# A second expert's first matrix is loaded one unit earlier, and two steps beside it change places

## The chip, the cores and the metric

The kernel runs on one core of one Trainium2 chip. The metric is device microseconds of one execution, from launch to end; several runs are taken and their median is compared. A profile is one further execution, recorded instruction by instruction. Engines are named PE (TensorE), DVE (VectorE), ACT (ScalarE), POOL (GpSimd) and SP (SyncE, which here only issues DMAs).

## What is computed

Attention with a compressive memory feeds two mixture-of-experts layers, one after the other. All tensors are float32, N is 2304 tokens, D 512, F 1024, and each layer has 8 experts. The first layer sends each token to one expert, the second to two; the cut below leaves the attention out.

```python
def _moe_ref(x, modality_id, w_gate, modality_bias, w1, w2):
    logits = x @ w_gate + modality_bias[modality_id]
    e_idx = np.argmax(logits, axis=1)
    ...
    for e in range(E):
        mask = e_idx == e
        h = np.maximum(x[mask] @ w1[e], 0.0)
        out[mask] = gate_w[mask, None] * (h @ w2[e])
    return out

def _moe2_ref(x, w_gate, w_noise, noise, w1, w2):
    noisy_logits = x @ w_gate + np.log1p(np.exp(x @ w_noise)) * noise
    top2 = np.argpartition(-noisy_logits, 2, axis=1)[:, :2]
    ...
    for e in range(E):
        for k in range(2):
            mask = top2[:, k] == e
            h = np.maximum(x[mask] @ w1[e], 0.0)
            out[mask] += top2_w[mask, k, None] * (h @ w2[e])
    return out

x = attn_out as (B*S, 512); x = _moe_ref(x, ...); return _moe2_ref(x, ...)
```

## The kernel before

The attention fills the first quarter of the span. Its instructions are ordered by a planner (class Tasks), and unit 0 of the first layer is planned in with them. From unit 1 on the order on every engine is that in which the Python code stands.

A **unit** of the first layer is 256 tokens of one expert (`full`). Both weights of an expert are 2 MB each. They are loaded raw (tiles w1r and w2r), and every float32 operand is split into a high and a low part: ACT casts the high one (w1h, w2h, xh), and DVE or POOL subtracts it to get the low one (w1l, w2l, xl). A product is then three matmuls per block (lines 718 to 720 and 728 to 730). The first product goes through eight blocks f of 128 hidden columns. The second goes through two token tiles t and four quarters q of the hidden columns; a quarter is six matmuls of 512 columns. In a unit the parts of the next unit's w1 are split during the second product (`split_w1`, one call per quarter), and the next tokens are gathered from DRAM by POOL and transposed by PE (`rows`, which calls `xsplit`: four transposes, ACT's xh, DVE's xl, and before a pair also ACT's unsplit copy xf).

**Between unit 1 and unit 2** stands `pair`: two halves t of 128 tokens each, of two experts, with unsplit float32 weights and tokens (tile xf). The first half uses w1r and w2r; the second half uses weights of another expert, wb1 and wb2. wb1 lies where unit 1 holds w2h and wb2 where it holds w2l. While the second half runs, w1r is loaded with unit 2's w1 and split. The code has four pairs, each inside an `If` on a register that counts them. In this run the first pair is done; the branch of the second is taken on every engine and jumps over the code of the other three. At the end of the jump each engine adds to its semaphores what the skipped code would have added, and unit 2 waits for these.

**Ranking.** The outputs of each unit get the second layer's gate logits and a rank among the tokens of the same expert. This work (`logits`, `route2`) is for the unit before the one that runs. `route2` is a generator: each `pump(slot)` runs up to five pieces of it. Slots 0 to 7 are the blocks f of the first product, slots 8 to 15 the quarters of the second (slot 8+4t+q). After the routing mask A is made on DVE (line 916) the generator yields 1, and `pump` then does nothing until the slot GATE[1], which is 10; the next piece is PE's five small matmuls on A (lines 919 to 923).

In the pair the slots are counted likewise: 8t+q in the first product of half t, 8t+4+q in the second.

Of the kernel before, what the change touches and what calls it, by code (L numbers as in the profile page):

```python
# [291 lines left out]

EARLY=256; CH=(C2-DEAD)//2
OLP=8
LSLOT=(0,1,3); GATE={1:10,2:99}; PUMP=5
LSLOT2=(0,1,2); GATE2={1:6,2:10}; PUMP2=8
AREAS=(9216,9216,5120,10240,8192,GB*XW,2*XW,512)

# [9 lines left out]
class Moe:  # L308
# [41 lines left out]
    def blocks(s, nc, c, areas):  # L350

        def T(j, o, w, name, dt=FT):
            assert o+w<=AREAS[j]
            return nc.alloc_sbuf_tensor_at(name,[128,w],dt,offset=nc.lookup_mloc(areas[j]).addr+4*o).ap()
        cut=lambda j,o,w,name,n,dt=FT:[T(j,o+i*w,w,name+str(i),dt) for i in range(n)]
        V=lambda a,k: a.rearrange('p (k w) -> p k w',k=k)
        K0,K1,X,HL,W2,G,X1,OL=range(8)
        s.w1r=V(T(K0,0,4096,'w1r'),KD); s.w2r=V(T(K0,4096,4096,'w2r'),KF); s.os=cut(K0,8192,512,'os',2)
        s.w1h=V(T(K1,0,4096,'w1h',FR),KD); s.w1l=V(T(K1,4096,4096,'w1l',FR),KD); s.yt=V(T(K1,8192,1024,'yt'),KD); s.rr=c.tile([128,4,256],FR,name='rrm')
        s.xh=V(T(X,0,2560,'xh',FR),KD); s.xl=V(T(X,2560,2560,'xl',FR),KD)  # L360
        s.w2h=cut(W2,0,512,'w2h',KF,FR); s.w2l=cut(W2,4096,512,'w2l',KF,FR)
        H=lambda n: [T(HL,o,KF*n,x+str(n),FR).rearrange('p (f c) -> p f c',f=KF) for o,x in ((0,'hh'),(5120,'hl'))]
        s.hidden=dict(l1=H(UT),l2=H(C2)); s.hh,s.hl=s.hidden['l1']
        s.xf=[V(T(X,o,2560,n),KD)[:,:,256:512] for o,n in ((0,'xf0'),(2560,'xf1'))]; s.hf=T(HL,0,KF*UT,'hf').rearrange('p (f c) -> p f c',f=KF)
        s.wb1=V(T(W2,0,4096,'wb1'),KD); s.wb2=V(T(W2,4096,4096,'wb2'),KF)
        s.x1=V(T(X1,0,2*XW,'x1'),2); s.ol2=V(T(OL,0,512,'ol2',FR),4); s.gs=cut(G,0,XW,'gs',GB); s.gn_=s.on_=0
        s.room=lambda o,w,dt: T(G,2*XW+o,w,'room%d'%o,dt); s.room1=lambda o,w,dt: T(X,o,w,'roox%d'%o,dt)
        t=KF*UT; s.tail=[T(HL,t,NT*128,'tl',FR),T(HL,5120+t,NT*3*COLS,'tr',FR),T(HL,5120+t+NT*3*COLS,NT*COLS,'to')]; s.ob=T(HL,5120,5120,'ob')
        s.kv=[T(X,2560,2560,'k0'),T(HL,0,2560,'k1')]; s.vs=[T(X,0,2560,'v0'),T(HL,2560,2560,'v1')]
        s.mask=T(G,2*XW,800,'mask'); s.mzs=T(G,2*XW+800,520,'mzs')  # L370
        s.bufs=dict(q=cut(HL,5120,512,'q',4),qb=cut(HL,7168,512,'qb',2),pts=cut(HL,8192,1024,'pts',2)+cut(W2,3328,1024,'ptx',1),
            sm=cut(W2,0,576,'sm',4),ph=cut(W2,2304,512,'ph',2),p=cut(W2,4352,640,'p',4),os=[T(K1,8192,512,'oc')],x=cut(W2,6912,512,'x',2),
            mo=cut(X1,0,512,'mo',2),xt=[T(OL,0,512,'xt')],l=cut(G,2*XW+1320,32,'l',3))
# [70 lines left out]
    def tasks(s, Q, A, w1, w2):  # L444
# [240 lines left out]
        Q.add(P+14,POOL,100,lambda:nc.gpsimd.memset(s.x1[:,:,D:],0.0),b3['x_add']+end)  # L685
        Q.add(P+14,POOL,300,lambda:nc.gpsimd.memset(s.rr[:,:,4*NC2:].bitcast(FT),0.0))

    def load_w(s, raw, w, e, eng=None):
        src=(w[bass.ds(e,1)] if not isinstance(e,int) else w[e:e+1]).rearrange('o (c p) f -> p (o c) f',p=128)
        (eng or s.nc.sync).dma_start(raw,src)  # L690
# [114 lines left out]
    def full(s, wk, ps, w1, w2, u):  # L805
        nc=s.nc; V=nc.vector
        e=s.expert(1,0) if u==1 else s.expert(0,u-1); s.load_w(s.w1r,w1,e)
        s.finish(); s.x1_out(s.np*2+2 if u==2 else col(u-1),2)
        s.chain=s.route2(wk,ps,u-1,2); s.hold=0
        nc.gpsimd.tensor_copy(s.nz[:,1],s.nz[:,0])  # L810
        for f in range(KF):
            s.mm1(ps,f,0,UT)
            if u==1: s.late(f)
            elif f==1: s.behind()
            if u>=NSTAT-1:
                if f==1:
                    last=s.last[:,u-1:u]
                    V.tensor_scalar(s.nx[:,0],s.M2[:,0,0:2],float(S0),0.0,op0=OP.add,op1=OP.max)
                    V.tensor_scalar(s.nx[:,1],s.nx[:,0],float(N),last,op0=OP.add,op1=OP.mult)
                    V.tensor_add(s.nxi,s.nx[:,1],s.gn[:,u-1])  # L820
                    V.tensor_scalar(s.run[:,0:1],last,float(EARLY),s.run[:,0:1],op0=OP.mult,op1=OP.max)
                if f==2: g=[s.gather(s.xd[:N+col(u-1)*128],s.nxi[:,t:t+1]) for t in range(2)]
            elif f==(7 if u==1 else 0): g=[s.gather(s.xd[:N],(s.gsi[:,0] if u==1 else s.gni[:,u-1])[:,t:t+1]) for t in range(2)]
            if f in LSLOT: s.logits(wk,ps,1+LSLOT.index(f))
            s.split_w(s.w2r,s.w2h,s.w2l,f,nc.vector if f<3 else nc.gpsimd)
            if f>LSLOT[2]: s.pump(f)
            if f==5: nc.gpsimd.tensor_copy(s.gwc,s.gws[:,col(u)+1:col(u)+2])
            if f==7: s.split_w1(0,nc.gpsimd)
        s.load_w(s.w2r,w2,e)
        for t in range(2):  # L830
            for q in range(4):
                y=s.mm2(ps,t*128,range(2*q,2*q+2),y if q else None)
                i=4*t+q
                if i<7: s.split_w1(i+1,nc.vector if i in (1,3,6) else nc.gpsimd)
                if i in ((3,5) if u==1 else (1,3)): s.rows(ps,i//4 if u==1 else i//2,g[i//4 if u==1 else i//2],s.xf[0] if u==1 else None)
                if t==1 and q==1: s.logits(wk,ps,0)
                s.pump(8+i)
                if i==6: s.kept(col(u),2)
            if not t: nc.scalar.activation(s.x1[:,0,:D],y,AF.Copy,scale=s.gws[:,col(u):col(u)+1])
        s.settle(y)  # L840
    def pair(s, wk, ps, w1, w2, p):


        nc=s.nc; V=nc.vector; G=nc.gpsimd; c0=HC+2*p
        e=s.expert(1,p+1); eb=s.expert(1,NP2+1+p)
        s.load_w(s.wb1,w1,eb)
        s.finish(); s.x1_out(c0-2,2)
        s.load_w(s.wb2,w2,eb)
        s.chain=s.route2(wk,ps,NF+p,2); s.hold=0
        G.tensor_copy(s.nz[:,1],s.nz[:,0])  # L850
        xf=s.xf[p%2]; g=[]
        for t,(a1,a2) in enumerate(((s.w1r,s.w2r),(s.wb1,s.wb2))):
            cs=slice(t*128,t*128+128)
            for q in range(4):
                if q%2==0: h=ps.tile([128,4,128],FT,name='h')
                for f in (2*q,2*q+1):
                    for k in range(KD): nc.tensor.matmul(h[:,f%4],a1[:,k,f*128:f*128+128],xf[:,k,cs],start=k==0,stop=k==KD-1)
                if q%2: nc.scalar.activation(s.hf[:,2*q-2:2*q+2,cs],h,AF.Relu)
                if t==0:
                    if q==1: s.behind(); g=[s.gather(s.xd[:N],s.gsi[:,p+1,j:j+1]) for j in range(2)]  # L860
                    if q in LSLOT: s.logits(wk,ps,1+LSLOT.index(q))
                if t and q:
                    for f in (2*q-2,2*q-1): s.split_w1(f,V if f%2 else G)
                if t or q>=LSLOT[2]: s.pump(8*t+q)
            if t==0: s.load_w(s.w1r,w1,e)
            y=ps.tile([128,512],FT,name='y')
            for q in range(4):
                for f in (2*q,2*q+1): nc.tensor.matmul(y,s.hf[:,f,cs],a2[:,f],start=f==0,stop=f==KF-1)
                if t:
                    if q==0:  # L870
                        for f in (6,7): s.split_w1(f,V if f%2 else G)
                elif q%2: s.rows(ps,q//2,g[q//2],s.xf[(p+1)%2])
                if t and q==0: s.logits(wk,ps,0)
                s.pump(8*t+4+q)
                if not t and q==1: G.tensor_copy(s.gwc,s.gws[:,c0+1:c0+2])
                if t and q==2: s.kept(c0,2)
            if not t: nc.scalar.activation(s.x1[:,0,:D],y,AF.Copy,scale=s.gws[:,c0:c0+1])
            if t==0: s.load_w(s.w2r,w2,e)
        s.settle(y)
# [287 lines left out]
```

## Time and profile before

| | us |
|---|---|
| median of 3 runs | 987.15 |
| lowest, highest | 986.49, 991.69 |
| the profiled execution | 984.86 |
| its span, first to last instruction | 983.1 |
| PE busy in the span | 943.0 |
| DVE busy | 555.5 |
| ACT busy | 488.2 |
| POOL busy | 353.2 |

Times below are microseconds from the start of the span of the profiled execution. Unit 1 runs from 248.8 to 284.6, the pair from there to 317.8, unit 2 after it. In the timeline views a row has the start, the time busy, the engine, the line of the kernel, the operation, the tiles written and read, the shapes and the count; a bracket at its end tells how long the engine stood idle before it and which instruction released it. A busy time runs over the start of the next instruction where an engine pipelines, so the cost of one instruction in a row of equal ones is the distance of two starts.

### The profile page before, as it was taken

Reading aid. Unit: us, or ns where it says so; the run is one execution under the profiler, and the core shown is the slowest. Engines: PE = TensorE matmul, PEld = TensorE weight load, DVE = VectorE, ACT = ScalarE, POOL = GpSimd, SP = SyncE. Lnnn points to the kernel's source line nnn. Section 1 sums busy time; section 2 is a strip of 40 time slices with the busy share of each in tenths; the row PEclk is TensorE's granted clock in tenths of the full one; section 3 lists DMA queues with packets and bytes.
Section 4 is the critical chain, followed back from the end, with each engine's and each line's share of the span. In section 5 each row is a group of like instructions: output and inputs, shape, how many; then the busy total and the mean of one; then the engine's idle time right before and its main releaser. Section 6 shows DMA issues by size and latency. Waiting matters only on the chain. (4 is left out here: it accounts for less than half of the span.)

```text
span 983.1 us, 18583 instructions
## 1 busy us (share of the span) xinstructions
PE 943.0 (96%) x6849; PEld 831.0 (85%) x6849; DVE 555.5 (56%) x1695; ACT 488.2 (50%) x1141; POOL 353.2 (36%) x420
## 2 busy tenths in 40 slices
PE   7999999999989999999997999999999999999994
PEld 5888888888875889888886999898989989898983
DVE  8777777789745577777775244243442424244320
ACT  6887878775433455555552244333342433343320
POOL 5222232244643567777765231121313021231111
PEclk9999999999989899999999999999999999999997
DMA  8345856262567555666655254536446354535112
GB/s 211 100 112 183 270 184 205 93 223 84 167 214 265 162 193 206 216 215 215 205 178 158 66 137 124 127 82 160 105 107 172 97 121 128 138 77 117 23 23 35
DMA packets 83840, 144.98 MB, mean 147 GB/s; under 512 B 14480, under 2 KB 32912, under 8 KB 83728
## 3 DMA queue, kind: packets, MB, share of 16 engines
q1 hardware_dynamic: 73168, 117.10, 36.4%
q0 software_dynamic: 10560, 26.47, 13.6%
q8 instruction: 60, 0.98, 0.4%
q14 instruction: 52, 0.43, 0.1%
HBM read 111.65 MB, written 31.97 MB: 146 GB/s over the span
## 5 line engine op out<-in xcount | busy, mean ns | idle before, releaser
L718 PE MATMUL b<-xh,w1h 128*128 128x304 f32 (+3 forms) x800 | 240.0, 300 | 3.1 <-ACT xh L709 1.3
L719 PE MATMUL b<-xl,w1h 128*128 128x304 f32 (+3 forms) x800 | 238.2, 298 | 3.8 <-DVEq L788 3.5
L720 PE MATMUL b<-xh,w1l 128*128 128x304 f32 (+3 forms) x800 | 237.1, 296 | 0.0
L723 DVE SCALAR_TENSOR_TENSOR hl<-b,hh 128x304 fp32r<-128x304 f32 (+3 forms) x200 | 90.7, 454 | 207.1 <-ACT hh L721 205.4
L728 PE MATMUL b<-w2h,hh 128*128 128x512 f32 x464 | 188.7, 407 | 0.0
L730 PE MATMUL b<-w2h,hl 128*128 128x512 f32 x464 | 182.2, 393 | 0.0
L973 POOL DMA_INDIRECT out_dram<-os,l2s x40 | 62.8, 1571 | 331.5 <-ACT os L972 253.3
L729 PE MATMUL b<-w2l,hh 128*128 128x512 f32 x464 | 181.6, 391 | 0.0
L721 ACT ACTIVATE hh<-b 128x304 fp32r<-128x304 f32 (+3 forms) x200 | 81.8, 409 | 172.7 <-PE b L720 172.6
L718 PEld LDWEIGHTS b<-xh,w1h 128*128 128x128 f32 x800 | 152.7, 191 | 9.3 <-DVE hl L723 4.1
L719 PEld LDWEIGHTS b<-xl,w1h 128*128 128x128 f32 x800 | 152.7, 191 | 4.8 <-DVEq L788 3.7
L720 PEld LDWEIGHTS b<-xh,w1l 128*128 128x128 f32 x800 | 152.9, 191 | 0.0
L730 PEld LDWEIGHTS b<-w2h,hl 128*128 128x128 f32 x464 | 87.5, 189 | 19.5
L729 PEld LDWEIGHTS b<-w2l,hh 128*128 128x128 f32 x464 | 88.0, 190 | 15.5
L728 PEld LDWEIGHTS b<-w2h,hh 128*128 128x128 f32 x464 | 87.7, 189 | 15.4
L151 ACT ACTIVATE p<-sm,l 128x128 f32<-128x128 f32 (+4 forms) x144 | 84.1, 592 | 16.9 <-DVE l L147 16.9
L698 DVE TENSOR_TENSOR w1l<-w1r,w1h 128x512 fp32r<-128x512 f32 x84 | 71.3, 857 | 22.0 <-ACT w1h L697 21.8
L710 DVE TENSOR_TENSOR xl<-b,xh 128x512 fp32r<-128x512 f32 x56 | 38.6, 689 | 73.9 <-ACT xh L709 73.7
L693 ACT CAST w2h<-w2r 128x512 fp32r<-128x512 f32 x128 | 78.5, 613 | 0.0
L709 ACT CAST xh<-b 128x512 fp32r<-128x512 f32 x56 | 32.9, 587 | 87.7 <-PE b L708 87.7
L697 ACT CAST w1h<-w1r 128x512 fp32r<-128x512 f32 x128 | 74.7, 620 | 0.3 <-DMA w1r<-in_w_dram 0.3
L972 ACT ACTIVATE os<-b,l2w 128x512 f32<-128x512 f32 x40 | 27.7, 691 | 94.1 <-PE b L730 47.6
(460 smaller groups left out, 1511.4 us busy)
## 6 DMA issues: line engine op xcount, KB each, us to landing
w1r<-in_w_dram SPq DMA_DIRECT2D x18, 2048.0 KB, 9.6
w2r<-in_w_dram SPq DMA_DIRECT2D x18, 2048.0 KB, 9.2
xd<-gs SPq DMA_DIRECT2D x24, 260.0 KB, 3.7
xd<-x SPq DMA_DIRECT2D x10, 520.0 KB, 10.3
out_dram<-gs SPq DMA_DIRECT2D x19, 256.0 KB, 4.0
k<-in_k_dram SPq DMA_DIRECT2D x16, 256.0 KB, 4.3
q<-in_q_dram SPq DMA_DIRECT2D x16, 256.0 KB, 3.5
v<-in_v_dram SPq DMA_DIRECT2D x16, 256.0 KB, 4.4
```

The source lines that it names most:

```text
L151: s.nc.scalar.activation(s.P[b,i,u][:,lh*n:lh*n+n],s.SM[b,i,u][:,lh*n:lh*n+n],AF.Exp,scale=-1.0,bias=L[:,0,c:c+1],accum_out=L[:,1,c:c+1])
L693: nc.scalar.copy(hi[c],raw[:,c])
L697: nc.scalar.copy(s.w1h[:,:,fs],s.w1r[:,:,fs])
L698: eng.tensor_sub(s.w1l[:,:,fs],s.w1r[:,:,fs],s.w1h[:,:,fs].bitcast(FT))
L718: nc.tensor.matmul(h[:,:n],s.w1h[:,k,fs],s.xh[:,k,cs],start=k==0,stop=False)
L719: nc.tensor.matmul(h[:,:n],s.w1h[:,k,fs],s.xl[:,k,cs],start=False,stop=False)
L720: nc.tensor.matmul(h[:,:n],s.w1l[:,k,fs],s.xh[:,k,cs],start=False,stop=k==KD-1)
L721: def mm1_a(s, h, f, c0, n): s.nc.scalar.activation(s.hh[:,f,c0:c0+n],h[:,:n],AF.Relu)
L723: cs=slice(c0,c0+n); s.nc.vector.scalar_tensor_tensor(s.hl[:,f,cs],h[:,:n],0.0,s.hh[:,f,cs].bitcast(FT),op0=OP.max,op1=OP.subtract)
L728: nc.tensor.matmul(y,s.hh[:,f,cs],s.w2h[f],start=f==0,stop=False)
L729: nc.tensor.matmul(y,s.hh[:,f,cs],s.w2l[f],start=False,stop=False)
L730: nc.tensor.matmul(y,s.hl[:,f,cs],s.w2h[f],start=False,stop=f==KF-1)
```

## The change

- The pair's wb1 gets a place of its own: two tiles of two k-blocks each in area HL (at 2048 and 7168), where unit 1's first product keeps tables (tl, tr) that its ranking of the first layer has read by then. For the first pair its load, now two DMAs of 1 MB, is issued in unit 1 right behind the load of w2r. Later pairs load it where they did. wb2 stays where it was.
- In the pair's second half, the calls `split_w1(f)` for unit 2's w1 follow the two blocks f of the same q, where they followed one q later, and the last two came after the first quarter of the second product. Six of the eight subtractions go to DVE (two to POOL: f = 0 and 4), where it was four and four.
- Unit 1 pumps its ranking by GATE1, with 12 where GATE has 10.

```diff
-LSLOT=(0,1,3); GATE={1:10,2:99}; PUMP=5
+LSLOT=(0,1,3); GATE={1:10,2:99}; GATE1={1:12,2:99}; PUMP=5
...
-        s.wb1=V(T(W2,0,4096,'wb1'),KD); s.wb2=V(T(W2,4096,4096,'wb2'),KF)
+        s.wb1=[V(T(HL,o,2048,'wb1%d'%o),2) for o in (2048,7168)]; s.wb2=V(T(W2,4096,4096,'wb2'),KF)
...
+    def load_wb1(s, w, e):
+        src=w[bass.ds(e,1)].rearrange('o (c p) f -> p (o c) f',p=128)
+        for i,x in enumerate(s.wb1): s.nc.sync.dma_start(x,src[:,2*i:2*i+2])
...
-            if f>LSLOT[2]: s.pump(f)
+            if f>LSLOT[2]: s.pump(f,GATE1 if u==1 else GATE)
...
         s.load_w(s.w2r,w2,e)
+        if u==1: s.load_wb1(w1,s.expert(1,NP2+1))
...
-                s.pump(8+i)
+                s.pump(8+i,GATE1 if u==1 else GATE)
...
-        s.load_w(s.wb1,w1,eb)
+        if p: s.load_wb1(w1,eb)
...
-                if t and q:
-                    for f in (2*q-2,2*q-1): s.split_w1(f,V if f%2 else G)
+                if t:
+                    for f in (2*q,2*q+1): s.split_w1(f,V if f%4 else G)
...
-                if t:
-                    if q==0:
-                        for f in (6,7): s.split_w1(f,V if f%2 else G)
-                elif q%2: s.rows(ps,q//2,g[q//2],s.xf[(p+1)%2])
+                if not t and q%2: s.rows(ps,q//2,g[q//2],s.xf[(p+1)%2])
```

PE in unit 1, around the five ranking matmuls. b is a PSUM bank, hh, hl and w2h, w2l are the split operands of the second product, gs a gathered token tile and x the outputs whose logits are made. Before:

```order
L730 MATMUL b_157<-w2h_74,hl_86 128x512
...
L919 MATMUL b_161<-A_3437,trib 128x8
...
L728 MATMUL b_157<-w2h_75,hh_85 128x512
...
L730 MATMUL b_157<-w2h_76,hl_86 128x512
L708 MATMUL b_160<-ident,gs_98 128x128 x4
L728 MATMUL b_158<-w2h_69,hh_85 128x512
```

The same engine and place after the change (lines have moved by one to four):

```order
L733 MATMUL b_158<-w2h_76,hl_86 128x512
L711 MATMUL b_161<-ident,gs_99 128x128 x4
L731 MATMUL b_159<-w2h_69,hh_85 128x512
...
L733 MATMUL b_159<-w2h_70,hl_86 128x512
...
L920 MATMUL b_162<-A_3450,trib 128x8
...
L731 MATMUL b_159<-w2h_71,hh_85 128x512
...
L711 MATMUL b_160<-ident,gs_100 128x128 x4
L758 MATMUL b_161<-ident,x_95 128x128 x4
```

The ranking matmuls stood behind the third quarter of the first token tile. They stand now behind one more quarter of it, the first four gather transposes and one quarter of the second tile; the second gather's transposes and the logits' transposes of x follow one quarter later, as they did.

ACT in the pair's second half. w1h are the casts of unit 2's w1, hf the pair's hidden tile, d the ranking's difference of two logits, x an output tile. Before:

```order
L877 ACTIVATE x_94<-b_157,gws 128x512
L858 ACTIVATE hf<-b_155 128x4x128
L697 CAST w1h<-w1r 128x4x128 x4
L926 ACTIVATE d_3733<-d_3733 128x2
L858 ACTIVATE hf<-b_156 128x4x128
L697 CAST w1h<-w1r 128x4x128 x4
```

After:

```order
L878 ACTIVATE x_95<-b_158,gws 128x512
L700 CAST w1h<-w1r 128x4x128 x2
L862 ACTIVATE hf<-b_156 128x4x128
L700 CAST w1h<-w1r 128x4x128 x4
L927 ACTIVATE d_3749<-d_3749 128x2
L862 ACTIVATE hf<-b_157 128x4x128
L700 CAST w1h<-w1r 128x4x128 x2
```

Two casts, and with them the wait for unit 2's w1, stand now ahead of the first evacuation of hf, and six ahead of the second where it was four.

SP from unit 1's load of w2r on. Before, wb_92 is wb1 and wb_93 is wb2:

```order
L690 DMA w2r<-in_w_dram 128x8x512
L788 COMPARE_AND_BRANCH
...
L690 DMA wb_92<-in_w_dram 128x4x1024
L882 DMA xd<-x_94 128x2x520
...
L690 DMA wb_93<-in_w_dram 128x8x512
...
L690 DMA w1r<-in_w_dram 128x4x1024
```

After, wb_92 and wb_93 are the halves of wb1 and wb_94 is wb2:

```order
L693 DMA w2r<-in_w_dram 128x8x512
...
L690 DMA wb_92<-in_w_dram 128x2x1024
...
L690 DMA wb_93<-in_w_dram 128x2x1024
L791 COMPARE_AND_BRANCH
...
L883 DMA xd<-x_95 128x2x520
...
L693 DMA wb_94<-in_w_dram 128x8x512
...
L693 DMA w1r<-in_w_dram 128x4x1024
```

The 2 MB of wb1 left the stretch ahead of unit 2's w1r and stand in unit 1, ahead of the branch.

## Rows read from the trace of the kernel before

**Rows 1.** The page, busy time by engine: us, share of span, instructions.

```profile
PE 943.0 (96%) x6849; PEld 831.0 (85%) x6849; DVE 555.5 (56%) x1695; ACT 488.2 (50%) x1141; POOL 353.2 (36%) x420
```

**Rows 2.** Waits of PE: who for whom, us in total, times, longest.

```profile
PE b L919 <- DVE A L916: 5.6, 2, 4.5
PE b L719 <- DVEq L788: 3.5, 1, 3.5
```

**Rows 3.** Stretches of 1 us: PE, PEld, DVE, ACT, POOL busy, PEclk, DMA share, GB/s.

```profile
271.00:272.00 1.00, 0.00 (x0) 0.00 (x0) 1.00 (x1) 0.00 (x0) 1.00 (x2) 0.87 0.50 100
...
278.00:279.00 1.00, 1.00 (x5) 0.82 (x5) 0.20 (x1) 0.59 (x1) 0.00 (x0) 0.71 0.07 27
...
319.00:320.00 1.00, 0.00 (x0) 0.00 (x0) 0.61 (x1) 0.35 (x1) 0.20 (x1) 0.77 0.04 8
...
326.00:327.00 1.00, 1.00 (x9) 1.00 (x9) 0.49 (x1) 0.47 (x1) 0.00 (x0) 0.82 1.02 418
```

**Rows 4.** Timeline of PE in unit 1 and at the pair's start.

```profile
268.00 0.39 PE L730 MATMUL b<-w2h,hl 128*128 128x512 f32 x1
...
269.36 0.39 PE L730 MATMUL b<-w2h,hl 128*128 128x512 f32 x1
274.25 0.17 PE L919 MATMUL b<-A,trib 128*128 128x8 bf16 x1 [4.50 <-DVE A L916]
...
281.00 0.60 PE L708 MATMUL b<-ident,gs 128*128 128x128 f32 x4
...
284.62 1.95 PE L857 MATMUL b<-xf,w1r 128*128 128x128 f32 x16
```

**Rows 5.** Timeline of DVE in unit 1 and the pair.

```profile
268.41 5.34 DVE L913 TENSOR_TENSOR b<-ix,tabs 128x4 f32<-128x4 uint32 x1
...
275.78 0.69 DVE L698 TENSOR_TENSOR w1l<-w1r,w1h 128x512 fp32r<-128x512 f32 x1 [0.35 <-ACT w1h L697]
...
308.44 3.03 DVE L698 TENSOR_TENSOR w1l<-w1r,w1h 128x512 fp32r<-128x512 f32 x2 [5.21 <-ACT w1h L697]
...
318.65 0.96 DVE L946 TENSOR_TENSOR rrm<-b,val 128x768 fp32r<-128x768 f32 x1
```

**Rows 6.** Timeline of ACT in unit 1 and the pair.

```profile
279.52 0.59 ACT L776 COPY xf<-b 128x512 f32<-128x512 f32 x1 [0.76 <-DVE xl L710]
280.00 0.69 ACT L839 ACTIVATE x<-b,gws 128x512 f32<-128x512 f32 x1
...
307.27 2.18 ACT L697 CAST w1h<-w1r 128x512 fp32r<-128x512 f32 x4 [0.32 <-DMA w1r<-in_w_dram]
```

**Rows 7.** Timeline of POOL in unit 1 and the pair.

```profile
270.03 3.69 POOL L698 TENSOR_TENSOR w1l<-w1r,w1h 128x512 fp32r<-128x512 f32 x3
...
307.96 2.96 POOL L698 TENSOR_TENSOR w1l<-w1r,w1h 128x512 fp32r<-128x512 f32 x2 [12.95 <-ACT w1h L697]
```

**Rows 8.** Timeline of PE where unit 2 begins.

```profile
317.85 0.39 PE L718 MATMUL b<-xh,w1h 128*128 128x256 f32 x1 [0.45 <-PEq L788]
321.77 0.58 PE L719 MATMUL b<-xl,w1h 128*128 128x256 f32 x1 [3.54 <-DVEq L788]
```

**Rows 9.** DVE's sequencer at the end of the pair: count, ns, first to last start.

```profile
L788 DVEq COMPARE_BRANCH  x1: 67/67/67, 318.7 to 318.7; - x1
...
L788 DVEq EVENT_SEMAPHORE  x1: 21/21/21, 321.7 to 321.7; - x1
```

**Rows 10.** DMA issues in unit 1 and the pair: count, KB, us to landing.

```profile
w2r<-in_w_dram SPq DMA_DIRECT2D x1, 2048.0 KB, 9.4
...
w1r<-in_w_dram SPq DMA_DIRECT2D x1, 2048.0 KB, 13.4
```

**Rows 11.** Timeline of PE at two other places, in unit 0 and layer two.

```profile
239.99 0.17 PE L471 MATMUL b<-room,onesb 128*128 128x8 bf16 x1 [1.54 <-DVE room L583]
...
539.57 0.45 PE L718 MATMUL b<-xh,w1h 128*128 128x384 f32 x1 [1.30 <-ACT xh L709]
```

**Rows 12.** Stretches of 1 us in layer two, columns as in rows 3.

```profile
541.00:542.00 1.00, 1.00 (x6) 1.00 (x5) 0.00 (x0) 0.00 (x0) 0.81 (x1) 0.70 0.85 47
```

More of the change, by code (lines that the diff above doesn't have):

```diff
@@ L851, in pair @@
         xf=s.xf[p%2]; g=[]
-        for t,(a1,a2) in enumerate(((s.w1r,s.w2r),(s.wb1,s.wb2))):
+        for t,(a1,a2) in enumerate((([s.w1r[:,k] for k in range(KD)],s.w2r),([x[:,k] for x in s.wb1 for k in range(2)],s.wb2))):
             cs=slice(t*128,t*128+128)
@@ L856, in pair @@
                 for f in (2*q,2*q+1):
-                    for k in range(KD): nc.tensor.matmul(h[:,f%4],a1[:,k,f*128:f*128+128],xf[:,k,cs],start=k==0,stop=k==KD-1)
+                    for k in range(KD): nc.tensor.matmul(h[:,f%4],a1[k][:,f*128:f*128+128],xf[:,k,cs],start=k==0,stop=k==KD-1)
                 if q%2: nc.scalar.activation(s.hf[:,2*q-2:2*q+2,cs],h,AF.Relu)
```

## The prediction

> **What bounds the kernel now.** I read the page's busy times first: PE is busy in 943.0 of 983.1 us [rows 1], so only what PE waits for, or does at the lower clock, can be won. Second, the waits of PE: the two longest that the change can touch are the ranking matmul of line 919, which waits for the mask A from DVE (4.50 of the 5.6 us are in unit 1), and the first low-part product of unit 2, which waits 3.5 us for DVE's sequencer at the end of the pair [rows 2]. Third, the granted clock around both. It falls from 2.4 to 1.2 GHz inside each wait and stays there after PE is back: a stretch's mean of 0.87 puts the fall at 271.74, one of 0.71 the return at 278.58; at the pair's end 0.77 and 0.82 give 319.54 and 326.36 [rows 3]. PE resumes at 274.25 [rows 4] and at 321.77 [rows 8]. It works 4.33 and 4.59 us at half rate, which costs half of that, 2.17 and 2.30.
>
> So the two places cost 4.50 + 2.17 + 3.54 + 2.30 = 12.5 us. This is the most that the change can give.
>
> **Why PE waits there.** In unit 1 DVE's tiny add of line 913 lasts 5.34 us, from 268.41 to 273.75, while POOL subtracts w1 parts without a pause until 273.72 [rows 5, 7]; A follows at 274.2. At the pair's end DVE starts its last instruction at 318.65 [rows 5], takes the branch over the three skipped pairs at 318.7, and its semaphore comes at 321.7: 3.0 us of jump [rows 9]. PE is there at 317.85 [rows 8]. DVE is late because it cannot start on unit 2's w1 before 308.44 [rows 5]: the load lands 13.4 us after its issue [rows 10], ACT's first cast starts with it at 307.27 [rows 6], and DVE's and POOL's subtractions then hold each other up (two of DVE's take 3.03 us, one alone 0.69) [rows 5, 7].
>
> **GATE1, 12 for 10.** One quarter of the second product is 269.36 - 268.00 = 1.36 us, four transposes about 0.43 (0.60 with their pipelined end) [rows 4]. PE puts a quarter, the transposes of the first gather and another quarter before the ranking matmuls: 1.36 + 0.43 + 1.36 = 3.15 us. What these need is ready: the low parts of w2 are done by 270.0, and the gathers were issued before 268. DVE and POOL have the same work up to A, so A still comes at 274.2, and of 4.50 us 1.35 stay.
>
> The cost is downstream. The logits' transposes of x come 1.36 + 0.43 us of PE work after the ranking, at 276.2. Their input on ACT stands behind xf, which waits for DVE's xl, which now stands behind A and two w1 parts. From A at 274.2: two parts 1.3, xl 0.7 [rows 5], xf 0.5 and x 0.7 [rows 6] give 277.3, so a new wait of 1.1 us; bounds 0.4 (if one part runs before A) and 1.8 (if a third stands ahead). The rest of the ranking ends on DVE by about 283.5, and its next matmul stands 3.9 us into the pair, at 284.3: nothing, with 0.8 us to spare.
>
> Whether the clock still falls decides 2.17 us. After a single wait of 1.54 us, in unit 0, PE went on at 2.4 GHz; in layer two, where a wait of 1.30 us was the second of two close together, the clock did fall, at 541.4 (mean 0.70) [rows 11, 12]. Waits of 1.35 and 1.1 lie between the two cases. I take no fall, narrowly, because neither reaches the single 1.54 and most of 3 us of work lies between them. Sum for unit 1: 4.50 - 1.35 - 1.1 + 2.17 = **4.2 us**; 2.0 if the clock falls.
>
> **wb1 beside unit 1.** The load is 2 MB either way. It goes behind w2r, which lands 9.4 us after its issue at 270.1 [rows 10], at 279.5, and is first needed 9.2 us into the pair, at 289.6 now; wb1 follows in the same queue and has some 18 us to the second half. Neither is waited for. Its place holds ranking tables that PE read last at 264. The wait of SP for that is over, so w2r, x1 and wb2 behind it in the queue are not held. Cost nothing; if the two loads shared the bandwidth evenly both would be there by about 286, still in time. On SP the step puts one register load and two issues ahead of the branch, where SP now only waits for unit 1's end. On POOL the ranking's copies now end the unit, so the gathers for unit 2 leave some 1.8 us later in the pair; they have about two us to spare. That is nothing too, and 0.5 at most if they miss it.
>
> The gain is in the queue: unit 2's w1r no longer has wb1 ahead of it. Its landing goes from 13.4 us towards the 9.4 of a load with an empty queue [rows 10]. wb2 is still ahead, so I take 10: w1r is there 3.4 us earlier in the pair, at 303.8 on the old trace's clock. ACT comes free at about 304.4, so the cover ends there.
>
> **Parts one quarter earlier, six on DVE.** (Times with one decimal here and above are from the same timelines as rows 4 to 8.) From 304.4 ACT casts parts 0 and 1, the first hf when PE has its two quarters (306.3), then parts 2 to 5 until 309.1. DVE subtracts 1, 2, 3, 5 until about 310.6 (0.69 each, and up to 1.3 behind each of POOL's two, since a POOL part takes 1.23 [rows 7]). Then d and exp, hf at 311 to 311.6, parts 6 and 7 until 313.4, 3.0 us of ranking and logits: DVE's last instruction starts at 316.0 instead of 318.65. Bounds: 314.6 if no subtraction waits for POOL's; 318.1 if w1r lands as late as now. The second half of hf is needed at 313.5 and is there at 311.6; the first is needed at 309.9 and is there at 307. So the casts ahead of hf cost nothing while w1r lands before 308.3.
>
> With the jump of 3.0 us DVE's semaphore comes at 319.05, and PE goes on 2.7 us earlier than 321.77; 0.8 us of waiting stays, which by the single wait of 1.54 us keeps the clock up: 2.7 + 2.30 = **5.0 us**. Ends: 0.55 (w1r late, clock falls) and 5.84 (no wait).
>
> **The sum.** 4.2 + 5.0 = 9.2 us, no other stretch changes. The profiled execution would go from 984.86 to 975.7. It lies 2.3 us under the median of the runs, and the runs differ mostly by one at 991.69, so I take the difference from the median: 987.15 - 9.2 = **978.0**.
>
> **Rivals.**
> (a) The clock falls at one of the two places nevertheless. For it speaks layer two, where two short waits were enough [rows 11, 12]; 9.2 - 2.2 = 7.0, 980.1 us.
> (b) The pair's end does not move: SP issues wb1 no earlier than before, because it waits for unit 1's last product, or DVE's tail hangs on hf and exp and not on w1r. Then the change does there nearly nothing, 4.2 to 4.7 us are won in all, 982.7. Against it speaks that the area's last reader is at 264.
> (c) Both waits go altogether, 987.15 - 12.5 = 974.7. It needs DVE 1.5 us earlier still.
> (d) Slower, by one mechanism: POOL holds DVE as it does now at 268.41, for 5.34 us over several of its instructions, and not for the 1.3 us of one. The new order gives it three places: POOL's parts 5 and 6 run back to back before the pair, and its two parts meet DVE's six in the pair. Two holds in the pair, 4.0 us more each, start DVE's last instruction at 324.0, 5.4 us later than now. One before the pair takes 5.3 - 0.8 = 4.5 us at line 949 and about 2.2 of clock from the 4.2 won. Together 5.4 + 2.5 = 7.9, and 995.0 us. It decides once POOL runs without a gap for over 3 us beside a DVE instruction with two SBUF inputs. Against it: POOL's runs there are of two parts at most, 2.5 us.
>
> On (d) the Trainium skill has a rule, "SBUF — State Buffer", section "Who interferes with whom": a VectorE instruction with two SBUF inputs and a GpSimd instruction that reads SBUF exclude each other, and the first to issue holds the shared port for its whole instruction. By that rule a meeting costs at most one POOL part, as in the forecast; the trace disagrees, since the add of line 913 outlasted several POOL instructions [rows 5, 7], and the measurement decides. That is why (d) keeps a chance.
>
> **Chances.** Forecast 0.46, (a) 0.26, (b) 0.16, (c) 0.07, (d) 0.05. Half a per cent, 4.9 us, is about what a measurement of this kernel can tell from no change. Forecast, (a) and (c) lie beyond it, less a little for the lower end of (a): faster 0.77. (b) lies within, and takes that little: same 0.18; slower is (d), 0.05. The range of 8 in 10 runs from (c) to a little behind (b): 974.7 to 983.5.
>
> **What would show it.** In the new trace PE's wait before the ranking matmuls in unit 1 should be 1 to 2 us, with a new one of about 1 us before the logits' transposes, and a clock of 1.00 from 271 to 280. ACT's first cast of unit 2's w1 should start about 19.7 us after the pair's start (now 22.7), DVE's branch should come about 31.4 us after it (now 34.1), and PE's wait for DVE's sequencer should be under 1.5 us, with the clock at 1.00 behind it. A clock of 0.50 at either place is (a); an unchanged distance from the pair's start to DVE's branch is (b); a DVE instruction of over 3 us in the pair is (d). The forecast is wrong if A moves, or if another wait of over 1 us appears in the pair.

## The result

The changed kernel takes 976.95 us (median of six runs, 976.01 to 980.08), the kernel before 987.86 in the same comparison: a ratio of 0.989, 95% interval 0.987 to 0.991, which is 10.9 us less (8.7 to 12.6). Run once more in another job it gave 0.9885 (0.987 to 0.990), which is 11.4 us (9.7 to 13.1). Times of different jobs are not compared below, only ratios to the runs of before that were taken with them, since before itself had medians from 983.9 to 990.6 us. The forecast was 978.0, or 9.2 us less, with a range of 974.7 to 983.5.

The profiled execution of the changed kernel took 980.08 us, the longest of its six. The page's busy times, then the waits of PE (us in total, times, longest; DVEq is DVE's sequencer), which answer to [rows 1, 2]:

```profile
PE 941.9 (96%) x6849; PEld 828.6 (85%) x6849; DVE 554.9 (57%) x1697; ACT 487.9 (50%) x1141; POOL 349.1 (36%) x418
```

```profile
PE b L920 <- DVE A L917: 2.4, 2, 1.4
...
PE b L758 <- ACT x L843: 0.8, 1, 0.8
...
PE b L722 <- DVEq L791: 0.3, 1, 0.3
```

The wait of 4.5 us before the ranking matmuls is down to 1.4, a new one of 0.8 stands before the logits' transposes, and the 3.5 us at unit 2 are 0.3. The timeline of PE at these places, which answers to [rows 4, 8]; the first row is the start of unit 1, L861 the start of the pair:

```profile
250.84 0.28 PE L721 MATMUL b<-xh,w1h 128*128 128x256 f32 x1
...
276.37 0.17 PE L920 MATMUL b<-A,trib 128*128 128x8 bf16 x1 [1.37 <-DVE A L917]
...
279.38 0.66 PE L758 MATMUL b<-ident,x 128*128 128x128 f32 x4 [0.83 <-ACT x L843]
...
282.62 1.95 PE L861 MATMUL b<-xf,w1r 128*128 128x128 f32 x16
...
316.57 0.38 PE L722 MATMUL b<-xl,w1h 128*128 128x256 f32 x1 [0.35 <-DVEq L791]
```

Stretches of 1 us behind the three waits, columns as in [rows 3] (the granted clock is the third number from the end):

```profile
276.00:277.00 1.00, 0.63 (x7) 0.59 (x7) 0.97 (x4) 0.00 (x0) 0.00 (x0) 1.00 0.99 360
...
280.00:281.00 1.00, 1.00 (x6) 0.81 (x5) 1.00 (x1) 0.93 (x2) 1.00 (x1) 1.00 1.02 381
...
317.00:318.00 1.00, 1.00 (x11) 1.00 (x10) 0.00 (x0) 0.00 (x0) 0.94 (x1) 1.00 0.50 83
```

The clock stays at 2.4 GHz in both places. From the start of unit 1 to the start of layer two the changed kernel takes 9.15 us less: 4.04 in unit 1 (31.78 for 35.82), 3.20 from the pair's start to unit 2's first low product (33.95 for 37.15), 1.91 behind it, where before ran at 1.2 GHz. Ahead of unit 1 the changed kernel's profile is 2.04 us longer than that of before, with a wait of 2.14 us in the attention and a fall of the clock at 223.85 that before has not. In layer two it is some 2.4 us longer: there an expert takes 56.33 us in before and in eight of the experiments, and 56.3 to 57.2 here, but also 56.3 to 57.3 in the kernel before with one pair in its code, which has none of the change, and 56.3 to 57.1 in the other three kernels of that job. None of the instructions that the change moves stands in either stretch. Why an expert takes longer in some executions was not pursued.

DVE, ACT and POOL of the changed kernel, to be read against [rows 5 to 7]:

```profile
270.46 5.41 DVE L914 TENSOR_TENSOR b<-ix,tabs 128x4 f32<-128x4 uint32 x1
...
313.37 0.96 DVE L947 TENSOR_TENSOR rrm<-b,val 128x768 fp32r<-128x768 f32 x1
```

```profile
302.23 1.14 ACT L700 CAST w1h<-w1r 128x512 fp32r<-128x512 f32 x2
```

```profile
270.82 1.30 POOL L697 TENSOR_TENSOR w2l<-w2r,w2h 128x512 fp32r<-128x512 f32 x1
272.07 3.76 POOL L701 TENSOR_TENSOR w1l<-w1r,w1h 128x512 fp32r<-128x512 f32 x3
```

The tiny add still lasts 5.4 us beside POOL's four subtractions: the gate did not make A earlier (25.5 us after the start of unit 1 in both kernels), it gave PE other work. In the pair ACT's first cast comes 19.6 us after the pair's start (22.65 before) and has no wait for the load in its row; DVE's last instruction starts 30.75 us after it (34.03).

### The profile page after: what moved, and what is told of

It is laid out like the page before. It is cut to its first block, busy times and chain, and to the rows that moved or that the text cites. A ratio compares the mean times of both kernels' runs of the same rounds, so it can differ in the third digit from the quotient of the medians.

```text
span 978.4 us, 18585 instructions
## 1 busy us (share of the span) xinstructions
PE 941.9 (96%) x6849; PEld 828.6 (85%) x6849; DVE 554.9 (57%) x1697; ACT 487.9 (50%) x1141; POOL 349.1 (36%) x418
```

## The experiments

All twelve in one table, with the kernel before. Unit 1 and the pair are lengths in the profile of each, from the first product of unit 1 to the pair's, and from there to unit 2's first low product; "DVE last" is the start of DVE's last instruction after the pair's start; the wait is PE's for DVE's sequencer at unit 2. The ratio is that of the runs, with its 95% interval.

| kernel | unit 1 | pair | DVE last | wait | ratio to before |
|---|---|---|---|---|---|
| before | 35.82 | 37.15 | 34.03 | 3.54 | 1 |
| changed | 31.78 | 33.95 | 30.75 | 0.35 | 0.989 (0.987 to 0.991) |
| gate alone | 31.77 | 37.48 | 34.53 | 3.87 | 0.996 (0.9945 to 0.997) |
| changed without the gate | 35.79 | 33.76 | 30.76 | 0.16 | 0.994 (0.993 to 0.996) |
| early load alone | 36.23 | 36.54 | 33.58 | 2.94 | 1.000 (0.999 to 1.001) |
| split order alone | 35.82 | 36.16 | 33.15 | 2.49 | 0.999 (0.998 to 1.001) |
| gate 11 | 33.64 | 33.73 | 30.76 | none | 0.991 (0.990 to 0.993) |
| four parts on POOL | 31.78 | 35.08 | 31.89 | 1.47 | 0.991 (0.990 to 0.9925) |
| no hold | 29.80 | 33.77 | 30.74 | 0.17 | 0.987 (0.986 to 0.989) |
| no hold, gate 10 | 30.93 | 34.01 | 30.85 | 0.32 | 0.988 (0.987 to 0.990) |
| hold of two | 30.43 | 33.82 | 30.77 | 0.21 | 0.986 (0.984 to 0.9875) |
| before, one pair in the code | 36.36 | 32.73 | 34.08 | none | 0.994 (0.992 to 0.995) |
| changed, again | 31.77 | 33.77 | 30.75 | 0.17 | 0.9885 (0.987 to 0.990) |
| no hold, again | 30.76 | 33.83 | 30.76 | 0.23 | 0.987 (0.985 to 0.988) |

### Which part gains what

Four kernels with parts of the change. The gate alone, added to before:

```diff
-LSLOT=(0,1,3); GATE={1:10,2:99}; PUMP=5
+LSLOT=(0,1,3); GATE={1:10,2:99}; GATE1={1:12,2:99}; PUMP=5
...
-            if f>LSLOT[2]: s.pump(f)
+            if f>LSLOT[2]: s.pump(f,GATE1 if u==1 else GATE)
...
-                s.pump(8+i)
+                s.pump(8+i,GATE1 if u==1 else GATE)
```

> The kernel before with GATE1 (12 for 10 in unit 1) and nothing else. Theory (the parts are independent): unit 1 ends 4.0 us sooner, as it did in the changed kernel (35.8 to 31.8 us); the join at unit 2 keeps its 3.5 us wait and its fall to 1.2 GHz; the time is 4.0 us under that of before, ratio 0.996. Rival (coupled): POOL's copies of the ranking now end the unit, the gathers for unit 2 leave 1.8 us later and the join's wait grows by as much; 2.2 us under before or less.

0.996 is 3.9 us, and unit 1 lasts 31.77 us as in the changed kernel, with the same two waits of 1.37 and 0.83; the join at unit 2 keeps its wait and its fall of the clock. The wait is 0.33 us longer than before (3.87), far from the 1.8 us of the rival. The theory holds.

The changed kernel without it (GATE1 at 10):

> The changed kernel with GATE1 put back to 10. Theory: unit 1 lasts 35.8 us again with a wait of 4.5 us at the ranking matmuls and a stretch at 1.2 GHz; the join's wait is 0.35 us with the clock at 2.4 GHz; 5.1 to 5.5 us under before, ratio 0.9945. Rival (coupled): the longer unit 1 gives the loads more time, and the join gains more than in the changed kernel, 6 us or more under before.

0.9942 is 5.7 us, and the wait at unit 2 is 0.16. The two halves add up: 3.9 and 5.7 are 9.6, against 10.9 and 11.4 of the whole in its two comparisons. Within these intervals they are independent, as the prediction took them.

The join was then taken apart into the load and the order of the splits. The load alone is the changed kernel without the gate and with

```diff
-                if t:
-                    for f in (2*q,2*q+1): s.split_w1(f,V if f%4 else G)
+                if t and q:
+                    for f in (2*q-2,2*q-1): s.split_w1(f,V if f%2 else G)
...
-                if not t and q%2: s.rows(ps,q//2,g[q//2],s.xf[(p+1)%2])
+                if t:
+                    if q==0:
+                        for f in (6,7): s.split_w1(f,V if f%2 else G)
+                elif q%2: s.rows(ps,q//2,g[q//2],s.xf[(p+1)%2])
```

> The changed kernel with GATE1 at 10 and with the splits of unit 2's w1 in their old order (one quarter later, four on DVE and four on POOL): only the place and the early load of wb1 are left. Theory (the load lets DVE start, the order lets it end): ACT's first cast follows the first hf at once, DVE's last instruction starts 1.0 to 1.6 us later than in the changed kernel, the wait at unit 2 is 1.4 to 2.0 us; 1.5 us under before if the clock falls there, 3.8 if it does not. Rival 1 (the load is all of it): wait 0.35, 5.3 under before. Rival 2 (the order is all of it): no gain.

The order alone is the same edit the other way, made in the kernel before:

> The kernel before with the splits one quarter earlier and six of them on DVE, and nothing else. Theory: w1r still lands 13.4 us after its issue behind wb1, ACT's casts wait for it and the first hf stands behind them; DVE's last instruction starts at most 0.6 us sooner, and the clock falls; within 0.7 us of before. Rival 2 (the order is all of it): the wait at unit 2 goes to 0.35 and 5.3 us are gained. Rival 3: the casts hold up hf and PE waits for it in the pair, 1 us or more slower than before.

Neither gains anything that the runs can tell (1.000 and 0.999, with intervals that reach 0.002 from one at most), while the two together gain 5.7 us. ACT's timeline shows why. The load alone:

```profile
307.02 0.60 ACT L862 ACTIVATE hf<-b 128x512 f32<-128x512 f32 x1 [2.00 <-PE b L861]
307.51 0.61 ACT L700 CAST w1h<-w1r 128x512 fp32r<-128x512 f32 x1
```

The order alone:

```profile
307.44 1.14 ACT L697 CAST w1h<-w1r 128x512 fp32r<-128x512 f32 x2 [3.08 <-DMA w1r<-in_w_dram]
308.49 0.59 ACT L858 ACTIVATE hf<-b 128x512 f32<-128x512 f32 x1
```

In the old order the first cast stands behind the first hf, and hf waits for PE until 307.0 (21.7 us into the pair): weights that land sooner lie there unused. In the new order without the load the cast waits 3.08 us for the weights, until 307.4 (22.8 us into the pair). Two conditions end at nearly the same time, so that the removal of either uncovers the other. My expectation for the load alone was wrong on this: I had DVE's last instruction 1.0 to 1.6 us later than in the changed kernel, and it was 2.8, with a wait of 2.94 for 1.4 to 2.0: I had the cast behind the first hf, but put too low what that costs. For the order alone I had DVE's last instruction at most 0.6 us sooner than before and a fall of the clock; it was 0.88 us sooner, and in the profile the wait is down to 2.49 and the clock stays at 2.4 GHz. Yet its runs range from 980.0 to 986.2 us at mean clocks of 0.990 down to 0.982, so in some of them the clock was low for longer than in the profile; where, no trace shows.

The order has a gain of its own that neither the prediction nor the expectations name. Before, and in the load alone, POOL's last subtraction meets DVE's table step of 512 elements; with the new order POOL is done by then. POOL and DVE of the kernel before:

```profile
316.46 1.27 POOL L698 TENSOR_TENSOR w1l<-w1r,w1h 128x512 fp32r<-128x512 f32 x1
```

```profile
316.52 1.76 DVE L943 TENSOR_TENSOR ol<-io,ri 128x512 fp32r<-128x512 f32 x1
```

In the changed kernel:

```profile
312.31 0.68 DVE L944 TENSOR_TENSOR ol<-io,ri 128x512 fp32r<-128x512 f32 x1
```

The 1.08 us are a third of the 3.28 us by which DVE's last instruction comes sooner in the changed kernel.

### How long POOL holds DVE

Four subtractions on POOL in the pair where the changed kernel has two:

```diff
-                    for f in (2*q,2*q+1): s.split_w1(f,V if f%4 else G)
+                    for f in (2*q,2*q+1): s.split_w1(f,V if f%2 else G)
```

> The changed kernel with four of the eight subtractions in the pair on POOL (f = 0, 2, 4, 6) where it has two. Theory (DVE and POOL hold each other up by one instruction at a time): DVE's last instruction starts 0.5 to 1.5 us later, the wait at unit 2 grows from 0.35 to about 1.0 and the clock stays; 0.7 us over the changed kernel. Rival (POOL holds DVE over several of its instructions): a DVE instruction of over 3 us in the pair, the clock falls at unit 2, 4 us or more over the changed kernel.

DVE, then POOL, then PE:

```profile
304.44 3.03 DVE L701 TENSOR_TENSOR w1l<-w1r,w1h 128x512 fp32r<-128x512 f32 x2 [0.99 <-ACT w1h L700]
```

```profile
303.97 2.95 POOL L701 TENSOR_TENSOR w1l<-w1r,w1h 128x512 fp32r<-128x512 f32 x2 [1.06 <-ACT w1h L700]
```

```profile
316.15 0.39 PE L722 MATMUL b<-xl,w1h 128*128 128x256 f32 x1 [1.47 <-DVEq L791]
```

DVE's two took 1.35 and 1.76 us, where one alone takes 0.69: each lost one POOL instruction at most, even beside two that stand back to back; POOL's two took 1.28 and 1.73, so the engines took turns. DVE's last instruction came 1.14 us later and the wait grew by 1.12, with the clock up. The theory, and the upper part of its range for DVE (0.5 to 1.5); the wait is longer than the 1.0 expected. Rival (d) of the prediction does not happen here, though POOL's 2.95 us end just short of the 3 us that it names.

For the add of unit 1 the opposite is true. In "no hold" unit 1's parts 0 to 4 and 7 are subtracted by DVE behind A, and POOL keeps 5 and 6:

```diff
-            if f==7: s.split_w1(0,nc.gpsimd)
+            if f==7 and u>1: s.split_w1(0,nc.gpsimd)
...
-                if i<7: s.split_w1(i+1,nc.vector if i in (1,3,6) else nc.gpsimd)
+                if i<7 and u>1: s.split_w1(i+1,nc.vector if i in (1,3,6) else nc.gpsimd)
...
                 s.pump(8+i,GATE1 if u==1 else GATE)
+                if i<7 and u==1:
+                    for f in ((0,1) if i==0 else (i+1,)): s.split_w1(f,nc.gpsimd if f in (5,6) else nc.vector)
```

> The changed kernel with unit 1's w1 parts given to DVE behind the mask A (parts 0 to 4 and 7; POOL keeps 5 and 6), so that POOL has one subtraction of w2 and no run of four beside the tiny add of line 914. Theory (POOL's run held the add for 5.41 us): the add takes under 1.5 us, A comes about 4 us sooner, the waits of 1.37 us before the ranking matmuls and of 0.83 us before the logits' transposes go; 2.2 us under the changed kernel. Rival (the add is slow for a reason of its own): the add still takes 5.4 us and the time is that of the changed kernel, or up to 2 us more, as DVE has three parts more behind A.

"Hold of two" is this kernel with part 3 left on POOL too:

```diff
-                    for f in ((0,1) if i==0 else (i+1,)): s.split_w1(f,nc.gpsimd if f in (5,6) else nc.vector)
+                    for f in ((0,1) if i==0 else (i+1,)): s.split_w1(f,nc.gpsimd if f in (3,5,6) else nc.vector)
```

> The same with part 3 left on POOL: POOL runs one subtraction of w2 and one of w1 back to back beside the add, where the changed kernel has four of them and the kernel without the hold one. Theory (the hold lasts until POOL's run ends): the add takes about 3.0 us, between 1.7 (one) and 5.4 (four), and A comes 1.3 us later than with one. Rival (a hold is one POOL instruction): the add takes 1.7 us or less.

DVE and POOL of "no hold":

```profile
268.70 1.71 DVE L916 TENSOR_TENSOR b<-ix,tabs 128x4 f32<-128x4 uint32 x1
```

```profile
268.10 0.95 POOL L704 DMA_INDIRECT gs<-xd,gsi  x1 [0.30 <-issue]
269.07 1.30 POOL L697 TENSOR_TENSOR w2l<-w2r,w2h 128x512 fp32r<-128x512 f32 x1
```

and of "hold of two":

```profile
271.13 2.95 DVE L916 TENSOR_TENSOR b<-ix,tabs 128x4 f32<-128x4 uint32 x1
```

```profile
271.50 1.30 POOL L697 TENSOR_TENSOR w2l<-w2r,w2h 128x512 fp32r<-128x512 f32 x1
272.75 1.29 POOL L701 TENSOR_TENSOR w1l<-w1r,w1h 128x512 fp32r<-128x512 f32 x1
```

One, two and four POOL subtractions beside it make the add 1.71, 2.95 and 5.41 us long, and each time it ends 0.04 us after the last of them (270.41 after 270.37, 274.08 after 274.04, 275.87 after 275.83). So the hold lasts as long as POOL's run. This cause, which the prediction read from one row, is shown. The run does not begin with a subtraction: in all three the add starts some 0.37 us ahead of the first one, while POOL is still at the DMA instruction of a gather (line 704 above), and the first subtraction is one of w2. Whether the gather matters was not tried. Why this add (four elements a partition) is let in between no two POOL instructions, and a subtraction of 512 is, stays open.

Without the hold A comes 3.7 us sooner and unit 1 lasts 29.8 us, 1.98 under the changed kernel (2.2 were expected: 0.36 us of the wait before the logits' transposes stay). The add, at 1.71 us, is a little over the 1.5 expected. With the hold gone, the gate was put back:

> The same with GATE1 back at 10, where the ranking matmuls stand 3.15 us earlier on PE. Theory (the gate only bridged the hold): A comes in time or up to 0.7 us late, the clock stays; 1.5 to 2.2 us under the changed kernel, as with 12. Rival (A is late for more than the hold): a wait of over 2 us before the ranking matmuls, and 2 us or more over the changed kernel.

In the profile with 10 no wait is left before the ranking or the logits, but a fall of the clock ahead of A, told of below, has put PE back by 1.56 us, and that hides one. A is made at the same time in both (21.8 us after the start of unit 1); DVE's last step of it and PE's first ranking matmul, with 10:

```profile
270.30 0.19 DVE L919 TENSOR_REDUCE A<-OH 128x16 bf16<-128x32 f32 x1
```

```profile
271.09 0.18 PE L922 MATMUL b<-A,trib 128*128 128x8 bf16 x1
```

Without the fall PE would be there 1.56 us sooner, at 269.5, and A at 270.5: an estimated wait of 1 us, in a unit 1 of 30.4 us beside 29.8 with 12. The runs agree: all four with 10 (972.86 to 974.22) lie above all four of "no hold" with 12 in the same job (971.45 to 972.24), medians 1.2 us apart, though the intervals of the two ratios overlap. So the gate mainly bridges the hold: without the hold it is worth about 1 us (0.6 by this estimate, 1.2 by the medians), and 4 with it.

"No hold" and the changed kernel were then run in one job:

> The changed kernel itself, as the measure for the two that come with it. Both theories: ratio to before 0.989, as before; in its profile unit 1 of 31.8 us, 34.0 us from the pair's start to the first low product of unit 2, the clock at 2.4 GHz in both places, the add of line 914 at 5.4 us.

> Unit 1's w1 parts 0 to 4 and 7 on DVE behind A, once more, beside the changed kernel. Theory (the hold is worth 2 us): unit 1 takes 29.8 us again, 2.0 us under the changed kernel, and the time of the runs stands 2 us under it. Rival (the 2 us are given back): unit 1 is shorter, and the time is that of the changed kernel within 0.5 us.

Medians of 979.16 for the changed kernel, 977.27 for "no hold" and 976.92 for "hold of two": 1.9 and 2.2 us less, in ratios 0.9885, 0.9866 and 0.9859, whose intervals overlap. The profile of "no hold" has 30.76 us for unit 1 this time, again with a fall of the clock ahead of A. I hold a further gain of about 2 us for likely and not for measured.

### The clock

GATE1 at 11, one quarter sooner:

> The changed kernel with GATE1 at 11: the ranking matmuls stand one quarter earlier on PE, A is made at the same time. The wait before them grows from 1.37 to 2.7 us, and the work between them and the logits' transposes grows by the same 1.36 us, so that the 0.83 us wait there goes. Theory (the clock falls some 2 us into a wait, as at 271.74 of before, whose wait began at 269.75): clock of 0.50 after the wait, 1.5 to 2.3 us over the changed kernel. Rival (the length of the wait does not decide it): clock 1.00, 0.3 us over the changed kernel.

PE, and three stretches:

```profile
273.06 0.17 PE L920 MATMUL b<-A,trib 128*128 128x8 bf16 x1 [2.71 <-DVE A L917]
```

```profile
272.00:273.00 1.00, 0.00 (x0) 0.00 (x0) 0.93 (x4) 0.00 (x0) 0.65 (x2) 1.00 0.99 362
273.00:274.00 1.00, 0.94 (x9) 0.81 (x9) 1.00 (x3) 0.00 (x0) 0.00 (x0) 1.00 1.03 393
274.00:275.00 1.00, 1.00 (x4) 0.81 (x3) 0.96 (x5) 0.16 (x1) 0.00 (x0) 0.52 1.03 381
```

The wait is 2.71 us as expected, the one at the logits is gone, and unit 1 is 1.86 us longer than with 12, though the one wait is only 0.51 us longer than the two together: the rest is the stretch at 1.2 GHz. So a good part of the gate's 4.0 us is the clock. The runs do not tell 11 from 12 (0.991 and 0.989, with intervals that overlap). But the fall came at 274.04, 1 us after PE was back at work, and not 2 us into the wait as I had it. The two waits of 12 (1.37 and 0.83) brought no fall there in any of the four profiles that have them; at unit 2 the clock fell behind waits of 2.94, 3.54 and 3.87 us and stayed up behind 2.49 and less, in one profile each.

### The jump

Before, with the code of the skipped pairs left out:

```diff
-            for p in range(NP2):
+            for p in range(1):
```

> The kernel before with the code of pairs 2 to 4 left out (they are skipped in this run in any case), so that there is no branch over them. Theory (the 3.0 us between DVE's branch and its semaphore are the jump over that code): unit 2's first low product does not wait for DVE's sequencer, or under 0.6 us, the clock stays at 2.4 GHz there, and 5 us or more are gained, as by the changed loads and splits. Rival (the 3 us are DVE's last instruction draining, or the cost of any end of a branch): the wait stays above 2 us.

PE where unit 2 begins, and the stretch around it:

```profile
318.48 0.68 PE L718 MATMUL b<-xh,w1h 128*128 128x256 f32 x1
318.99 0.28 PE L719 MATMUL b<-xl,w1h 128*128 128x256 f32 x1
```

```profile
319.00:320.00 1.00, 1.00 (x11) 1.00 (x10) 1.00 (x2) 0.69 (x1) 1.00 (x3) 1.00 0.00 0
```

PE does not wait for any sequencer, though DVE starts its last instruction at 34.08 us as late as before, and the clock stays up: 0.9936 is 6.3 us (5.1 to 7.6). The join's price was the branch over the skipped code and the semaphore behind it, which a late DVE reaches late; this kernel takes both away, so it does not tell the two apart. PE's own branch has a price too: unit 2's first high product starts 33.23 us after the pair's start in before (33.22 in the changed kernel), and 32.22 here, 1.0 us sooner. The wait of 3.54, the clock's 1.91 and this make 6.4 us, beside the 6.3 of the runs. The branch can be mostly hidden (the change, which keeps the 1.0) or left out (this kernel, which serves only this count of pairs).

## Why the prediction was right

**The total** was 9.2 us; the stretch that the change touches gave 9.15 in the profile, the runs 10.9 and 11.4, with the forecast inside the first interval (8.7 to 12.6) and 0.5 us below the second (9.7 to 13.1). The terms were off by up to 0.5 us each and made up for each other, so that the sum is as close as 0.1 us is luck. Why the runs gain 1 to 2 us more than the stretch stays open.

**Unit 1**, 4.2 against 4.04. The wait before the ranking was put at 1.35 and is 1.37; the new one at 1.1 and is 0.83; A did not move; the clock stayed at 2.4 GHz, which was the narrow choice against rival (a): it came out in all four profiles with these waits, but the two rows that it went by did not show why. What was mis-sized is the price of the low clock: 4.50 - 1.37 - 0.83 are 2.30, so 1.74 came from the clock, and not 2.17. "It works at half rate, which costs half of that" is the step that was off in size. Two starts of PE in before, at 1.2 GHz:

```profile
275.81 0.63 PE L728 MATMUL b<-w2h,hh 128*128 128x512 f32 x1
276.23 0.63 PE L729 MATMUL b<-w2l,hh 128*128 128x512 f32 x1
```

From 274.95 to 277.09 such starts stand 0.428 us apart in the mean, where at 2.4 GHz it is 0.227 [rows 4: 1.36 us for six]: 1.88 times as long, and for 256 columns 0.214 against 0.120, 1.78 times. By that the two stretches cost 2.0 each and not 2.17 and 2.30. In unit 1 that is still 0.3 more than the 1.74; 0.17 of it is that PE's pipelined end, which a next matmul would cover, shows before each wait (four transposes 0.60 for 0.43), and unit 1 now has two waits where it had one.

The reading of the hold was a little off: of POOL's run beside the add only the last three subtractions are of w1, and its first subtraction starts at 268.78, 0.37 us after the add.

**The join**, 5.0 against 3.20 + 1.91 = 5.11. ACT's first cast was put at 19.7 us and came at 19.6. DVE's last instruction was put at 31.4 and came at 30.75: DVE lost 0.7 us to each of POOL's two parts and not up to 1.3, and the steps behind the last part took 2.3 us, where the prediction has 2.6 (its 313.4 and 3.0 us would make 316.4, and it goes on with 316.0). The wait was 0.35 and not 0.8, so PE went on 3.2 us earlier and not 2.7. The clock's return was worth 1.91 and not 2.30, for the reason above. That the load and the order must go together is in the prediction only as the clause that the casts "cost nothing while w1r lands before 308.3"; what each does alone it does not say, and in the runs neither alone can be told from no change.

**Rivals.** (a) Neither place fell to 1.2 GHz in the changed kernel's two profiles. (b) The pair's end moved by 3.2 us. (c) The waits shrank to 1.37, 0.83 and 0.35, and did not go. (d) did not occur: on this the Trainium skill's rule ("SBUF — State Buffer", section "Who interferes with whom": the first to issue holds the port for its whole instruction) agrees with the four-part run, 1.35 and 1.76 us, and not with the add, 5.41, which started ahead of every subtraction that it waited out. The measurements decide: both kinds of meeting are in the same kernel, so a small chance for (d) was fair.

**What was free** proved free: no wait for wb1 or w2r appears, and the gathers that leave later are waited for by nobody on PE.

## What to carry to other kernels

When a stage waits for a load and also stands behind another step in the queue, look at both times: if they are close, one edit shows nothing and is easily thrown away, and here the two together gave the whole gain. A late tiny instruction is a reason to look at what its neighbour engine runs at that moment; to take the cause away (parts moved from POOL to DVE) left the bridge (the gate) worth about 1 us of its 4. A branch over skipped code cost 1.0 us on PE, which came early, and its full 3 us on DVE, which came late.

## What the hardware showed that was not expected

The same waits do not always bring the same clock. In layer two PE waits alike in two executions of the changed kernel: 1.30 us, some 4 us behind another wait, of 1.21 in the first and 1.35 in the second. The first execution, and a stretch behind it:

```profile
532.33 0.45 PE L721 MATMUL b<-xh,w1h 128*128 128x384 f32 x1 [1.30 <-ACT xh L712]
```

```profile
535.00:536.00 1.00, 1.00 (x4) 1.00 (x4) 0.00 (x0) 0.07 (x1) 0.73 (x1) 0.50 0.98 164
```

The second:

```profile
532.24 0.45 PE L721 MATMUL b<-xh,w1h 128*128 128x384 f32 x1 [1.30 <-ACT xh L712]
```

```profile
535.00:536.00 1.00, 1.00 (x7) 1.00 (x6) 0.29 (x1) 0.49 (x1) 0.82 (x1) 1.00 0.93 164
```

And in "no hold, gate 10" the clock fell in a stretch in which PE was busy throughout, with no wait over 0.67 us ahead of it; "no hold", with the same instructions up to there, stayed at 1.00:

```profile
263.22 0.87 PE L634 MATMUL b<-tr,tl 128*128 128x102 f32 x6 [0.67 <-DVE tl L657]
```

```profile
264.00:265.00 1.00, 1.00 (x9) 1.00 (x9) 0.97 (x5) 0.00 (x0) 1.00 (x3) 0.82 0.00 0
265.00:266.00 1.00, 1.00 (x6) 1.00 (x6) 0.93 (x3) 0.00 (x0) 0.67 (x1) 0.50 0.00 0
```

So a fall can be made likely or unlikely, but not foretold from one trace. In one job it is also most of the spread of the runs: the 24 runs of before there go from 980.8 us at a mean clock of 0.990 to 985.7 at 0.985, and a straight line through them has 0.57 us for each thousandth and leaves a fifth of their variance. In another job 11 runs of before do not follow the clock (988.7 us at 0.985, 992.2 at 0.987). The two stretches that the change took away (6.8 us each) are 0.007 of the mean clock, and in the second comparison it went from between 0.981 and 0.987 in the runs of before to between 0.991 and 0.994 with the change. What sets a fall where the waits are the same was not tried.
